# Moving the domain check of the weights from the first mixture into the second

## The chip, the cores and the metric

The kernel runs on one core of a Trainium2 chip. The metric is the device time of one execution in microseconds (us). The engines are TensorE (PE, with its weight loads PEld), VectorE (DVE), ScalarE (ACT), GpSimd (POOL) and SyncE (SP); in this kernel SP issues all DMAs, in the order of its own queue. Three runs of the kernel before gave a median of 1160.13 us (1159.07 to 1164.9).

## The reference

Three stages in float32: gated attention as a recurrence, and two mixtures of dense products.

```python
f = 1.0 / (1.0 + np.exp(-f_logit))              # 4 x 8 heads, 768 steps, 48 wide
state = f[:, :, t, :, None] * state + np.einsum('bhd,bhe->bhde', k[:, :, t], v[:, :, t])
y[:, :, t] = np.einsum('bhd,bhde->bhe', q[:, :, t], state)

h = x @ w_in                                    # x: 3072 x 384, w_in: 384 x 2048
x = (h * np.cos(h)) @ w_out                     # first mixture, w_out: 2048 x 384

xn = x / np.sqrt(np.mean(x * x, axis=-1, keepdims=True) + 1e-06) * rms_g
g, val = xn @ w_gate, xn @ w_val                # 384 x 1536 each
out = (g / (1.0 + np.exp(-g)) * val) @ w_out2   # second mixture, w_out2: 1536 x 384
```

The weights come as float64. The kernel reads them as 32-bit words and rebuilds each as two float32r parts by shifts. That holds only for magnitudes in a certain range, so every weight's upper word is also tested: this is the domain check. If a weight (or a gate product) is out of range, a general path at the end recomputes everything; with these inputs it does not run.

## The kernel before

Attention runs in 24 steps of 128 tokens, four pieces to a step. Both mixtures run over six blocks of 512 tokens, in slots. A slot of the first mixture takes one 128-wide slice of `w_in` (16 slots a block); one of the second takes a slice of the gate and value weights (12 a block). Slots are numbered through: 0 to 95 for the first mixture, 96 to 167 for the second. The pieces of attention lie in the slots of blocks 0 to 4 of the first mixture.

A slot of the first mixture is a chain over engines: nine matmuls into a bank (`m1_h`, L655), `kint` on ACT (L664), `wrap` on DVE (L670), the cosine on ACT (L676), `g` on DVE (L681), its two parts `gh` on ACT (L689) and `gl` on POOL (L697), and two slots later nine output matmuls (`m1_out`, L707). Banks alternate, so the matmuls of a slot wait for the `g` of two slots before. A slot of the second mixture has 18 matmuls (L805), `sg` on ACT (L814), `u` on DVE (L819), `uh` on ACT (L826), `ul` on DVE (L832) and 12 output matmuls of the slot before (L841).

The class `Decode` rebuilds weights. A unit is 128 x 384 weights: its words come by DMA into a `stage` tile (three buffers), ACT makes `wx` (L597), DVE joins the words in two steps (L609, L613), and ACT and POOL write the parts (L629, L630). The weights of the first mixture are decoded in the prologue and block 0, those of the second (36 units, `dec2`) in block 5 and in block 0 of the second mixture.

The domain check of one unit is one DVE instruction (L529), which folds the upper words into `wacc`:

```python
def domain(hi):
    nc.vector.scalar_tensor_tensor(
        out=wacc, in0=hi, scalar=1 << 30, in1=wacc, op0=ALU.bitwise_xor, op1=ALU.bitwise_and,
    )
```

For `w_in` and `w_out` the words are read a second time: `recheck` loads 32 units (L540) in slots 16 to 78 and checks each two slots later. For the 36 units of `dec2` the check follows L613. `count_ok` turns `wacc` into a flag, in slot 110.

What sets the order: `manual_schedule` keeps the order of the code in the prologue, in block 0, in block 5 (`blk5`) and from block 1 of the second mixture on (`ph1`). In blocks 1 to 4 of the first mixture (`mid`) and in block 0 of the second (`ph0`) a scheduler orders each engine's instructions by its own costs. Work that belongs to a slot number is put into tables: `post_at` (run at the key `po`), `dve_at` (at `dv`), `act_at`, `pe_at`. In `ph1` the keys run as `gv pe ok act sg dv u uh ul po out ev`, so on DVE `dv` stands ahead of `u`.

Per block the sums of squares go through memory: `ss_d` (L743), back as `ssc` (L745), and the inverse root is written as `ri_d` (L752), 512 values of 4 bytes. `norm` reads it back spread over the partitions (`rb`, L773) with `x2b` (L769) and scales on DVE (L780). The raw tiles of attention (f, k, q) come by L175 and L176 into three buffers and are turned on DVE (L180).

Of the kernel before, what the change touches and what calls it, by code (L numbers as in the profile page):

```python
# [32 lines left out]
def kernel(  # L33
# [15 lines left out]
    B, H, S, D = q.shape  # L49
# [7 lines left out]
    KD = DM // 128  # L57
    N1 = F1 // 128
    N2 = F2 // 128
# [3 lines left out]
    w_in_w, w_out_w, w_gate_w, w_val_w, w_out2_w = (  # L63
        w.bitcast(I32) for w in (w_in, w_out, w_gate, w_val, w_out2)
    )
    INV2PI = 1.0 / (2.0 * math.pi)

    # Attention runs in chunks of 128 tokens. With p(t) the running product of the gates in the
    # chunk and p_end its value at the chunk's end,
    #   y(t) = q(t) p(t)/p_end . [p_end S] + sum_{s<=t} (q(t) p(t)/p_end . k(s) p_end/p(s)) v(s).  # L70
    # Where p_end gets too small for that quotient the general path at the end recomputes
    # everything by the recurrence itself.
    # Dense products: every operand is the sum of two float32r parts. The weights come as the
    # words of float64; shifting an upper word left by 3 gives float32 bits of -|w| 2^128 (for
    # 2^-255 <= |w| < 1, what is outside goes to the general path), the lower word has the last
    # 3 bits.

    cpool = ctx.enter_context(tc.tile_pool(name="cpool", bufs=1))
    dpool = ctx.enter_context(tc.tile_pool(name="dpool", bufs=1, space=DRAM))
# [74 lines left out]
        for t in am + vtl + [Tz]:  # L154
            nc.gpsimd.memset(t, 0.0)

# [1 line left out]
    st = {}  # L158
    rawc = [0]

# [51 lines left out]
    def eng(x):  # L212
        return nc.vector if x == "V" else nc.gpsimd
# [94 lines left out]
    def att_bank():  # L308
        bc[0] += 1
        return bank[3 + bc[0] % 5] if bc[0] <= 5 * HEAD else bank[5 + bc[0] % 3]  # L310
# [4 lines left out]
    def copy(x):  # L315
        return nc.vector.tensor_copy if x == "V" else nc.scalar.copy

    def split(n, j):
        """Both parts of k and q of the pairs' heads j, one above the other."""
        kt, qt = st[n, "kt"], st[n, "qt"]  # L320
        top, bot, own = slice(0, D), slice(64, 64 + D), slice(64 * j, 64 * j + D)
        r = [copy(x) for x in OPT["rnd"]]
        if j == 0:
            r[0](out=ks[top], in_=kt[top])
            r[1](out=qs[top, 0], in_=qt[top])
            r[2](out=qs[bot, 0], in_=qt[top])
        else:
            r[3](out=ks[bot], in_=kt[bot])
            r[4](out=ks[top], in_=kt[bot])
            r[5](out=qs[bot, 0], in_=qt[bot])  # L330
            r[6](out=qs[top, 0], in_=qt[bot])
        eng(OPT["kl"][j]).tensor_tensor(
            out=ks[bot], in0=kt[own], in1=ks[own].bitcast(F32), op=ALU.subtract
        )
        eng(OPT["ql"][j]).tensor_tensor(
            out=qs[top, 1], in0=qt[own], in1=qs[own, 0].bitcast(F32), op=ALU.subtract
        )
# [70 lines left out]
    def ys(n):  # L408
        if True:
            t = att_bank()  # L410
            qt, vt, vt2 = st.pop((n, "qt")), st.pop((n, "v")), vtl[n % 2]
            inter = n % NCH > 0
            # Rows of x: 64 (i % 2) + 32 j + e of part i // 2 for e < 32, 16 (2 i + j) + e - 32 of
            # the last part for the others.
            for c in range(2):
                cs = slice(C * c, C * (c + 1))
                if inter:
                    for x in range(2):
                        i = 2 * c + x
                        nc.tensor.matmul(  # L420
                            t[64 * x:64 * x + 64, cs], Tz[:, i, 0:64], qt[:, i, :],
                            start=True, stop=False,
                        )
                for x in range(4):
                    i, j = divmod(4 * c + x, 2)
                    nc.tensor.matmul(
                        t[32 * x:32 * x + 32, cs], vt[:, 2 * i + j, 0:32],
                        am[j][:, C * i:C * (i + 1)], start=not inter, stop=True,
                    )
            if inter:  # L430
                for i in range(NP):
                    nc.tensor.matmul(
                        t[32 * i:32 * i + 32, 2 * C:3 * C], Tz[:, i, 64:96], qt[:, i, :],
                        start=True, stop=False,
                    )
            for j in range(2):
                for i in range(NP):
                    nc.tensor.matmul(
                        t[32 * i:32 * i + 32, 2 * C:3 * C], vt2[:, i, j:j + 2, :],
                        am[j][:, C * i:C * (i + 1)],  # L440
                        start=not inter and j == 0, stop=j == 1,
                    )
            st[n, "y"] = t
# [53 lines left out]
            Sn = st[n, "S"]  # L497
            nc.vector.tensor_tensor(out=Sn, in0=Sn, in1=z, op=ALU.add)

# [1 line left out]
    blocks = [(t0, 512) for t0 in range(0, NT, 512)]  # L501
    step_block = {}
    for j, (t0, n) in enumerate(blocks):
# [24 lines left out]
    def domain(hi):  # L528
        nc.vector.scalar_tensor_tensor(  # L529
            out=wacc, in0=hi, scalar=1 << 30, in1=wacc,  # L530
            op0=ALU.bitwise_xor, op1=ALU.bitwise_and,
        )

    def recheck_load(u):
        src = (w_in_w, w_out_w)[u % 2]
        R = src.shape[0] // 128
        words = src.rearrange("(p r) f -> p (r f)", r=R)
        n = 2 * KD * 128
        t = mp.tile([128, KD, 256], I32, tag="stage", name="stage", bufs=3)
        nc.sync.dma_start(  # L540
            out=t.rearrange("p c f -> p (c f)"), in_=words[:, n * (u // 2):n * (u // 2 + 1)]
        )
        return t[:, :, 1::2]

    class Decode:
        """Weights into pairs of float32r tiles, in steps that keep the engines apart."""

        def __init__(self, order, check):
            self.order, self.check = order, check
# [201 lines left out]
        nc.gpsimd.tensor_tensor(out=c, in0=c, in1=mh.to_broadcast([128, N // 128]), op=ALU.pow)  # L751
        nc.sync.dma_start(out=ri_d[t0:t0 + N].rearrange("(c p) -> p c", p=128), in_=c)  # L752

# [1 line left out]
    NB2 = NT // 512  # L755
    pairs2 = []
    o2 = [bank[0], bank[1], bank[2], bank[5]]
    pb = [(bank[6], bank[7]), (bank[3], bank[4])]
# [35 lines left out]
    pc = [0]  # L794
# [61 lines left out]
    mh = pp.tile([128, 1], F32, name="mh")  # L856

    def count_ok(b):
        """The partitions on which no gate product was too small and no weight out of range."""
        t = pp.tile([128, 4], F32, name="okt")  # L860
        ti = mp.tile([128, KD, 128], I32, tag="wx", name="oki", bufs=3)
        tf = mp.tile([128, KD, 128], F32, tag="stage", name="okf", bufs=3)
        nc.vector.tensor_scalar(
            ti, wacc, 26, 31, op0=ALU.logical_shift_right, op1=ALU.bitwise_and
        )
        nc.vector.tensor_scalar(tf, ti, 31.0, None, op0=ALU.is_equal)
        nc.vector.tensor_reduce(
            out=t[:, 0:1], in_=tf.rearrange("p c f -> p (c f)"), axis=AX.X, op=ALU.min
        )
        nc.vector.tensor_reduce(  # L870
            out=t[:, 1:2], in_=pall.rearrange("p n i -> p (n i)"), axis=AX.X, op=ALU.min
        )
        nc.vector.tensor_scalar(t[:, 2:3], t[:, 1:2], P_MIN, None, op0=ALU.is_ge)
        nc.vector.tensor_tensor(out=t[:, 3:4], in0=t[:, 0:1], in1=t[:, 2:3], op=ALU.mult)
        nc.vector.tensor_reduce(out=t[:, 1:2], in_=low, axis=AX.X, op=ALU.max)
        nc.vector.tensor_scalar(t[:, 2:3], t[:, 1:2], 0.0, None, op0=ALU.is_equal)
        nc.vector.tensor_tensor(out=t[:, 3:4], in0=t[:, 3:4], in1=t[:, 2:3], op=ALU.mult)
        nc.tensor.matmul(b[0:1, 0:1], t[:, 3:4], ones[:, 0:1], start=True, stop=True)
        nc.vector.tensor_copy(out=okn, in_=b[0:1, 0:1])
# [11 lines left out]
    if True:  # L891
# [72 lines left out]
        pe_at, act_at, post_at, dve_at = {}, {}, {}, {}  # L964

        def at(table, slot, fn, *a):
            table.setdefault(slot, []).append((fn, a))
# [7 lines left out]
        held = {}  # L975
# [5 lines left out]
        def set_(key, fn, *a):  # L981
            held[key] = fn(*a)

        def recheck(u, s):
            at(post_at, s, lambda: set_(("hi", u), recheck_load, u))
            at(dve_at, s + 2, lambda: domain(held.pop(("hi", u))))

        at(post_at, 12, lambda: nc.gpsimd.memset(ks.bitcast(F32), 0.0))
        at(post_at, 13, lambda: nc.gpsimd.memset(qs.bitcast(F32), 0.0))
        for u in range(2 * N1):  # L990
            recheck(u, N1 + 2 * u)

        def finish(j, s, short):
            at(act_at, s + (1 if short else 2), lambda: set_((j, "x2"), m1_evac, j))
# [15 lines left out]
        for j, (t0, N) in enumerate(blocks):  # L1010
# [3 lines left out]
            if final:  # L1014
# [15 lines left out]
                for u, key in enumerate(order2):  # L1030
# [3 lines left out]
                    else (w_gate_w if nm == "g" else w_val_w, None, 128 * i,  # L1034
                          lambda nm=nm, i=i: w2[nm, i])
                    for nm, i in order2
                ], True)
                norm(0, slot + 10)
            for i in range(N1):
                cur = []  # L1040
# [49 lines left out]
        for jj in range(NB2):  # L1090
# [4 lines left out]
            for i in range(N2):  # L1095
# [1 line left out]
                do = {  # L1097
                    "gv": lambda: m2_gv(jj, i),
                    "pe": lambda: run(pe_at, slot),
                    "ok": lambda: jj == 1 and i == 2 and count_ok(pb[pc[0] % 2][0]),  # L1100
                    "act": lambda: run(act_at, slot),
                    "t": lambda: jj == 0 and dec2.step_split(),
                    "x": lambda: jj == 0 and dec2.step_x(),
# [21 lines left out]
        stack2.close()  # L1125
    fast.close()

# [1 line left out]
    n_ok = nc.values_load(okn, min_val=0, max_val=128)  # L1129
    with tc.If(n_ok < 128):  # L1130
        general(
# [240 lines left out]
```

## Time and profile before

| | us |
|---|---|
| median of 3 runs | 1160.13 |
| profiled execution, span from the first to the last instruction | 1158.3 |
| PE busy | 1026.2 (89%) |
| DVE busy | 740.1 (64%) |
| ACT busy | 471.1 (41%) |
| POOL busy | 442.7 (38%) |

The page gives no time of the profiled execution beside its span; the median of the runs is 1.8 us above it, and that difference is taken for what lies around the span. The shares are means over stages that differ: the page's slices show DVE at 5 to 9 tenths over the first 65% of the span and at 2 to 3 tenths behind, while PE is at 9 tenths behind. In the stretches below, blocks are cut where the first L655 of a block starts (180.3, 291.7, 397.3, 498.0 and 591.6 us); 680.3 is the last `g` of the first mixture, and from 749.5 PE runs without a gap to 1147.6.

### The profile page before, as it was taken

How to read it: one execution, taken by the hardware profiler on the slowest of the kernel's cores; microseconds unless marked ns; L12 is line 12 of the kernel's file. 1: busy time of each engine (PE TensorE's matmuls, PEld its weight loads, DVE VectorE, ACT ScalarE, POOL GpSimd, SP SyncE). 2: the span in 40 equal slices, each digit the busy share in tenths (PEclk: the TensorE clock that was granted, in tenths of full speed). 3: DMA queues.
4: the chain of work that ended last, by engine and by line, in shares of the span. 5: the costliest groups of instructions: out<-in, count | busy, mean ns of one | idle time of the engine just before them, and what ended most of it. 6: DMA issues, size and time to landing. Idle time of an engine off the chain costs nothing.

```text
span 1158.3 us, 15494 instructions
## 1 busy us (share of the span) xinstructions
PE 1026.2 (89%) x5720; PEld 828.2 (71%) x5720; DVE 740.1 (64%) x1093; ACT 471.1 (41%) x841; POOL 442.7 (38%) x460
## 2 busy tenths in 40 slices
PE   6687789887987878998999787999999999999997
PEld 5455557665765666776776566788888888888886
DVE  6888999977895999887658699722322322323222
ACT  3355656444553555554555454422221222222211
POOL 3466676653654464656547556410000100001000
PEclk8697989998999899999999898999999999999999
DMA  9893353325425433530022434201010010100000
GB/s 160 175 181 104 91 144 100 91 26 131 126 60 98 141 113 100 89 88 1 2 68 69 105 121 147 83 18 47 1 64 1 1 65 1 64 1 1 28 1 31
DMA packets 108208, 84.90 MB, mean 73 GB/s; under 512 B 50518, under 2 KB 93526, under 8 KB 108124
## 3 DMA queue, kind: packets, MB, share of 16 engines
q1 hardware_dynamic: 108124, 83.82, 29.3%
q8 instruction: 47, 0.77, 0.3%
q14 instruction: 37, 0.30, 0.1%
HBM read 74.33 MB, written 9.46 MB: 72 GB/s over the span
## 4 chain that ended last, share of the span: by engine, by line
PE 43%; DVE 32%; DMA 9%; issue 8%; ACT 5%; SPq 1%; POOL 1%; DVEq 0%; ACTq 0%; POOLq 0%
PE bank L805 23%; PE bank L841 12%; PE bank L707 3%; DVE wrap L670 3%; DVE wx L609 3%; DVE g L681 3%; DVE wx L613 3%; DVE wacc L529 3%; PE bank L655 3%; DMA stage<-in_moe_w_out_dram 2%; DMA raw<-in_f_logit_dram 2%; DVE ft L271 1%; DVE E L253 1%; DVE ft L180 1%; DVE kt L180 1%
## 5 line engine op out<-in xcount | busy, mean ns | idle before, releaser
L707 PE MATMUL bank<-gh,wo 128*128 128x512 f32 x576 | 210.2, 420 | 2.3 <-ACT gh L689 2.3
L819 DVE SCALAR_TENSOR_TENSOR u<-bank,sg 128x512 f32<-128x512 f32 x72 | 49.7, 690 | 242.3 <-PE bank L805 240.8
L697 POOL TENSOR_TENSOR gl<-g,gh 128x512 fp32r<-128x512 f32 x96 | 133.4, 1390 | 124.0 <-ACT gh L689 119.0
L789 POOL TENSOR_TENSOR xl<-x2b,xh 128x512 fp32r<-128x512 f32 x18 | 24.5, 1366 | 314.3 <-ACT xh L788 314.3
L707 PEld LDWEIGHTS bank<-gh,wo 128*128 128x128 f32 x576 | 114.2, 198 | 31.8 <-issue 3.6
L707 PE MATMUL bank<-gl,wo 128*128 128x512 f32 x288 | 120.4, 418 | 10.7 <-POOL gl L697 10.7
L805 PE MATMUL bank<-xh,wo 128*128 128x512 f32 x360 | 122.8, 395 | 0.0
L814 ACT ACTIVATE sg<-bank 128x512 f32<-128x512 f32 x72 | 43.1, 598 | 168.9 <-PE bank L805 168.9
L676 ACT ACTIVATE wrap<-wrap,cb 128x512 f32<-128x512 f32 x96 | 69.4, 723 | 85.1 <-DVE wrap L670 84.5
L826 ACT CAST uh<-u 128x512 fp32r<-128x512 f32 x72 | 44.7, 621 | 142.8 <-DVE u L819 142.6
L689 ACT CAST gh<-g 128x512 fp32r<-128x512 f32 x96 | 59.4, 619 | 92.0 <-DVE g L681 69.5
L670 DVE SCALAR_TENSOR_TENSOR wrap<-bank,kint 128x512 f32<-128x512 f32 x96 | 65.4, 681 | 31.1 <-ACT kint L664 30.8
L832 DVE TENSOR_TENSOR ul<-u,uh 128x512 fp32r<-128x512 f32 x72 | 54.5, 757 | 44.7 <-ACT uh L826 44.7
L805 PEld LDWEIGHTS bank<-xh,wo 128*128 128x128 f32 x360 | 67.6, 188 | 14.6
L707 PEld LDWEIGHTS bank<-gl,wo 128*128 128x128 f32 x288 | 57.3, 199 | 26.1 <-POOL gl L697 15.6
L681 DVE SCALAR_TENSOR_TENSOR g<-bank,wrap 128x512 f32<-128x512 f32 x96 | 65.4, 681 | 16.1 <-ACT wrap L676 14.5
L841 PE MATMUL bank<-wo,uh 128*128 128x384 f32 x288 | 73.7, 337 | 0.0
L664 ACT ACTIVATE kint<-bank,cb 128x512 int32<-128x512 f32 x96 | 65.5, 683 | 15.6 <-PE bank L655 15.5
L805 PE MATMUL bank<-xl,wo 128*128 128x512 f32 x180 | 71.0, 394 | 0.0
L529 DVE SCALAR_TENSOR_TENSOR wacc<-stage,wacc 128x384 int32<-128x384 int32 x68 | 62.1, 913 | 11.5 <-DMA stage<-in_moe_w_in_dram 11.3
L841 PEld LDWEIGHTS bank<-wo,uh 128*128 128x128 f32 x288 | 52.6, 188 | 3.2 <-ACT uh L826 0.2
L613 DVE SCALAR_TENSOR_TENSOR wx<-stage,wx 128x384 int32<-128x384 int32 x52 | 51.8, 996 | 1.2
(376 smaller groups left out, 2506.9 us busy)
## 6 DMA issues: line engine op xcount, KB each, us to landing
stage<-in_moe_w_out_dram SPq DMA_DIRECT2D x44, 384.0 KB, 3.6
stage<-in_moe_w_in_dram SPq DMA_DIRECT2D x16, 384.0 KB, 3.9
v_sb<-in_v_dram SPq DMA_DIRECT2D x24, 192.0 KB, 4.2
x_d<-x SPq DMA_DIRECT2D x6, 768.0 KB
stage<-in_moe_w_gate_dram SPq DMA_DIRECT2D x12, 384.0 KB, 3.1
stage<-in_moe_w_val_dram SPq DMA_DIRECT2D x12, 384.0 KB, 3.3
x2b<-x_d SPq DMA_DIRECT2D x6, 768.0 KB, 5.0
out_dram<-ob SPq DMA_DIRECT2D x24, 192.0 KB, 2.0
```

The lines of the kernel that those rows point to most:

```text
L529: nc.vector.scalar_tensor_tensor(out=wacc, in0=hi, scalar=1 << 30, in1=wacc, op0=ALU.bitwise_xor, op1=ALU.bitwise_and,)
L613: nc.vector.scalar_tensor_tensor(out=f, in0=hi, scalar=-(1 << 29), in1=f, op0=ALU.bitwise_and, op1=ALU.bitwise_xor)
L664: nc.scalar.activation(out=kt, in_=hb[j, i], func=AF.Identity, scale=INV2PI * UNIT, bias=cb[:, 0:1])
L670: nc.vector.scalar_tensor_tensor(out=w, in0=hb[j, i], scalar=INV2PI * UNIT, in1=kt, op0=ALU.mult, op1=ALU.subtract)
L676: nc.scalar.activation(out=w, in_=w, func=AF.Sin, scale=2.0 * math.pi, bias=cb[:, 1:2])
L681: nc.vector.scalar_tensor_tensor(out=g, in0=hb.pop((j, i)), scalar=UNIT, in1=w, op0=ALU.mult, op1=ALU.mult)
L689: nc.scalar.copy(out=h, in_=g)
L697: e.tensor_tensor(out=l, in0=g, in1=h.bitcast(F32), op=ALU.subtract)
L707: nc.tensor.matmul(acc[m][:, 0:N], lw[:, cs], r, start=i == 0 and x == 0, stop=i == N1 - 1 and x == 2,)
L805: nc.tensor.matmul(t[y], l[:, 128 * kk:128 * (kk + 1)], r[:, kk, :], start=idx == 0, stop=idx == 3 * KD - 1,)
L832: nc.vector.tensor_tensor(out=l, in0=u, in1=h.bitcast(F32), op=ALU.subtract)
L841: nc.tensor.matmul(o2[tt][:, 0:DM], lu[:, cs], r, start=i == 0 and x == 0, stop=i == N2 - 1 and x == 2,)
```

## The change

All 68 checks are done in slots 108 to 157, which are blocks 1 to 4 of the second mixture and the first two slots of block 5. Each has a load of its own, of 384 KB from memory; `dec2` no longer checks, so the words of `w_gate`, `w_val` and `w_out2` are read twice. `count_ok` moves to slot 164. Line numbers behind the changed code are larger by 3. (The diff also empties comment lines.)

```diff
-    def recheck_load(u):
-        src = (w_in_w, w_out_w)[u % 2]
-        R = src.shape[0] // 128
-        words = src.rearrange("(p r) f -> p (r f)", r=R)
-        n = 2 * KD * 128
+    UNIT_W = 2 * KD * 128
+    units = [
+        (w, u) for w in (w_in_w, w_out_w, w_gate_w, w_val_w, w_out2_w)
+        for u in range(w.shape[0] * w.shape[1] // (128 * UNIT_W))
+    ]
+
+    def check_load(src, u):
+        words = src.rearrange("(p r) f -> p (r f)", r=src.shape[0] // 128)
         t = mp.tile([128, KD, 256], I32, tag="stage", name="stage", bufs=3)
         nc.sync.dma_start(
-            out=t.rearrange("p c f -> p (c f)"), in_=words[:, n * (u // 2):n * (u // 2 + 1)]
+            out=t.rearrange("p c f -> p (c f)"), in_=words[:, UNIT_W * u:UNIT_W * (u + 1)]
         )
         return t[:, :, 1::2]
...
-        def recheck(u, s):
-            at(post_at, s, lambda: set_(("hi", u), recheck_load, u))
-            at(dve_at, s + 2, lambda: domain(held.pop(("hi", u))))
-
...
-        for u in range(2 * N1):
-            recheck(u, N1 + 2 * u)
+
+        first = len(blocks) * N1 + N2
+        for n, (w, u) in enumerate(units):
+            s = first + n * (4 * N2) // len(units)
+            at(post_at, s, lambda n=n, w=w, u=u: set_(("hi", n), check_load, w, u))
+            at(dve_at, s + 2, lambda n=n: domain(held.pop(("hi", n))))
...
                     for nm, i in order2
-                ], True)
+                ], False)
...
-                    "ok": lambda: jj == 1 and i == 2 and count_ok(pb[pc[0] % 2][0]),
+                    "ok": lambda: jj == NB2 - 1 and i == 8 and count_ok(pb[pc[0] % 2][0]),
```

The scheduler of `mid` orders anew. On DVE in block 2 of the first mixture, where a step's q is done and the next step's f begins, stands before:

```order
L466 TENSOR_TENSOR xl_643<-bank_79,xh_642 128x3x128
L283 TENSOR_TENSOR qt<-qt,ft 128x512
L529 SCALAR_TENSOR_TENSOR wacc<-stage,wacc 128x384
L226 MEMSET ft 128x4
L180 STREAM_TRANSPOSE ft<-raw_128 128x4x4x32
```

and now:

```order
L466 TENSOR_TENSOR xl_643<-bank_79,xh_642 128x3x128
L283 TENSOR_TENSOR qt<-qt,ft 128x512
L226 MEMSET ft 128x4
L180 STREAM_TRANSPOSE ft<-raw_128 128x4x4x32
```

The check between the two steps is gone; the rest keeps its place. On SP in block 1, around the write of `ri_d` (L752, now L755), where raw_128 is the next step's f and raw_129 its k, stands before:

```order
L743 DMA ss_d<-ssr 1x512
L175 DMA raw_130<-in_q_dram 32x4x192
L176 DMA raw_130<-in_q_dram 32x4x160
L745 DMA ssc<-ss_d 128x4x1
L166 DMA v_sb<-in_v_dram 128x8x48
L175 DMA raw_128<-in_f_logit_dram 32x4x192
L752 DMA ri_d<-ssc 128x4x1
L176 DMA raw_128<-in_f_logit_dram 32x4x160
L175 DMA raw_128<-in_f_logit_dram 32x4x192
L176 DMA raw_128<-in_f_logit_dram 32x4x160
L540 DMA stage<-in_moe_w_in_dram 128x768
```

and now:

```order
L746 DMA ss_d<-ssr 1x512
L175 DMA raw_128<-in_f_logit_dram 32x4x192
L176 DMA raw_128<-in_f_logit_dram 32x4x160
L748 DMA ssc<-ss_d 128x4x1
L175 DMA raw_128<-in_f_logit_dram 32x4x192
L176 DMA raw_128<-in_f_logit_dram 32x4x160
L755 DMA ri_d<-ssc 128x4x1
L175 DMA raw_129<-in_k_dram 32x4x192
L176 DMA raw_129<-in_k_dram 32x4x160
```

Three of the four loads of f stood behind `ri_d`; now all four stand ahead of it and k follows it. On DVE in block 1 of the second mixture stands before:

```order
L832 TENSOR_TENSOR ul<-u,uh 128x512
L780 SCALAR_TENSOR_TENSOR x2b<-x2b,g_sb,rb 128x512
L819 SCALAR_TENSOR_TENSOR u<-bank_81,sg 128x512
L832 TENSOR_TENSOR ul<-u,uh 128x512
L780 SCALAR_TENSOR_TENSOR x2b<-x2b,g_sb,rb 128x512
L819 SCALAR_TENSOR_TENSOR u<-bank_78,sg 128x512
```

and now:

```order
L835 TENSOR_TENSOR ul<-u,uh 128x512
L529 SCALAR_TENSOR_TENSOR wacc<-stage,wacc 128x384
L783 SCALAR_TENSOR_TENSOR x2b<-x2b,g_sb,rb 128x512
L822 SCALAR_TENSOR_TENSOR u<-bank_81,sg 128x512
L835 TENSOR_TENSOR ul<-u,uh 128x512
L529 SCALAR_TENSOR_TENSOR wacc<-stage,wacc 128x384 x2
L783 SCALAR_TENSOR_TENSOR x2b<-x2b,g_sb,rb 128x512
L822 SCALAR_TENSOR_TENSOR u<-bank_78,sg 128x512
```

One or two checks stand in each slot between the `ul` of the slot before and the `u` of the slot.

## Rows read from the trace of the kernel before

**Rows 1.** Windows by stage: start:end length, busy per engine (instructions), PE clock, DMA share, GB/s

```profile
180.30:291.70 111.40, 92.24 (x566) 70.10 (x565) 95.92 (x145) 54.08 (x99) 57.72 (x61) 0.91 0.38 88
291.70:397.30 105.60, 89.10 (x580) 68.51 (x579) 87.97 (x145) 50.25 (x91) 60.33 (x64) 0.94 0.42 99
397.30:498.00 100.70, 88.90 (x560) 68.64 (x559) 89.69 (x142) 53.90 (x99) 57.42 (x60) 0.95 0.45 108
498.00:591.60 93.60, 86.11 (x571) 66.41 (x570) 68.28 (x106) 48.91 (x86) 51.51 (x55) 0.98 0.08 22
591.60:680.30 88.70, 77.67 (x314) 59.78 (x313) 66.85 (x83) 49.78 (x87) 54.31 (x42) 0.94 0.33 93
680.30:749.50 69.20, 55.69 (x236) 45.72 (x235) 62.04 (x84) 31.79 (x60) 34.98 (x28) 0.93 0.41 129
749.50:1147.60 398.10, 397.74 (x1903) 346.83 (x1903) 113.81 (x161) 90.26 (x154) 21.61 (x17) 1.00 0.07 21
```

**Rows 2.** The same windows for line L529 alone: length, DVE busy (instructions)

```profile
180.30:291.70 111.40, 4.71 (x6) 0.91 0.38 88
291.70:397.30 105.60, 9.04 (x13) 0.94 0.42 99
397.30:498.00 100.70, 6.93 (x9) 0.95 0.45 108
...
591.60:680.30 88.70, 21.98 (x16) 0.94 0.33 93
680.30:749.50 69.20, 17.79 (x21) 0.93 0.41 129
```

**Rows 3.** Timeline of block 5: start, duration, engine, line, operation, [idle before <-releaser]

```profile
639.73 0.68 DVE L670 SCALAR_TENSOR_TENSOR wrap<-bank,kint 128x512 f32<-128x512 f32 x1
...
642.75 1.42 POOL L697 TENSOR_TENSOR gl<-g,gh 128x512 fp32r<-128x512 f32 x1 [2.06 <-ACT gh L689]
...
642.94 1.65 DVE L529 SCALAR_TENSOR_TENSOR wacc<-stage,wacc 128x384 int32<-128x384 int32 x1
...
644.51 0.68 DVE L670 SCALAR_TENSOR_TENSOR wrap<-bank,kint 128x512 f32<-128x512 f32 x1
```

**Rows 4.** Waits of PE in block 1, then in block 2: total, times, longest

```profile
PE bank L655 <- DVE g L681: 6.8, 2, 5.7
...
PE bank L655 <- DVE g L681: 12.5, 2, 9.6
```

**Rows 5.** Timeline of DVE in block 1, then in block 2

```profile
263.91 1.11 DVE L180 STREAM_TRANSPOSE ft<-raw 128x512 f32<-128x512 f32 x1 [7.25 <-DMA raw<-in_f_logit_dram]
...
370.36 0.56 DVE L529 SCALAR_TENSOR_TENSOR wacc<-stage,wacc 128x384 int32<-128x384 int32 x1 [10.69 <-DMA stage<-in_moe_w_in_dram]
```

**Rows 6.** Chain of waits at the end of block 4: start, length, what

```profile
587.61 2.07 PE bank L655 x9
589.68 2.10 PE bank L707 x9
```

**Rows 7.** Timeline of DVE in block 5, slots that also scale `x2b`

```profile
662.11 0.75 DVE L780 SCALAR_TENSOR_TENSOR x2b<-x2b,g_sb,rb 128x512 f32<-128x512 f32 x1 [7.35 <-DMA rb<-ri_d]
...
666.97 0.68 DVE L670 SCALAR_TENSOR_TENSOR wrap<-bank,kint 128x512 f32<-128x512 f32 x1
...
672.75 0.68 DVE L670 SCALAR_TENSOR_TENSOR wrap<-bank,kint 128x512 f32<-128x512 f32 x1
```

**Rows 8.** Waits of PE from 680.3 to 749.5 us

```profile
PE bank L841 <- DVE ul L832: 5.9, 3, 2.5
PE bank L841 <- ACT uh L826: 4.0, 2, 3.5
```

**Rows 9.** Timeline of DVE in the second mixture, around 940 us

```profile
934.61 0.69 DVE L819 SCALAR_TENSOR_TENSOR u<-bank,sg 128x512 f32<-128x512 f32 x1 [3.23 <-PE bank L805]
...
940.88 0.69 DVE L819 SCALAR_TENSOR_TENSOR u<-bank,sg 128x512 f32<-128x512 f32 x1 [4.20 <-PE bank L805]
```

**Rows 10.** DMA issues by line: count, KB each, median us to landing

```profile
stage<-in_moe_w_in_dram SPq DMA_DIRECT2D x16, 384.0 KB, 3.9
```

## The prediction

> **What bounds the kernel now.** I cut the span into stages first, since its mean shares hide them [rows 1]. From 749.5 to 1147.6 us PE is busy 397.74 of 398.10 us at a granted clock of 1.00, and DVE only 113.81: that stretch is bound by PE, and DVE has 284 us to spare. Ahead of it the picture turns. In blocks 1 to 3 of the first mixture DVE is busy for 83 to 89% of the time, PE idles for 12 to 19 us in each, and the clock is 0.91 to 0.95. From 680.3 to 749.5 us DVE is busy 62.04 of 69.20 us, and PE idles for 13.5. So time taken from DVE ahead of 749.5 can shorten the kernel, and time given to it behind can be free.
>
> The second view is the same cut for the check alone [rows 2]: 4.71, 9.04 and 6.93 us in blocks 1, 2 and 3, 21.98 in block 5 and 17.79 in block 0 of the second mixture. Block 4 has no check, and is the shortest of the four. The third is the timeline of block 5, where the order is that of the code [rows 3]: from one `wrap` to the next it is 4.78 us, and the last 1.57 of them (642.94 to 644.51) are the check, which holds the next `wrap` back. The fourth is who waits. In blocks 1 and 2 the longest wait of PE on `g` is 5.7 and 9.6 us [rows 4], and DVE itself had stood before for 7.25 us for a load of f and for 10.69 us for the load of a check [rows 5].
>
> **What is removed, stage by stage.** I count a gain only where PE waits for DVE.
>
> Block 1: six checks, 4.71 us. DVE is busy for 86% of the block, but other waits of PE remain, so I take half: 2.4. The wait for f: three of its four loads stood behind the write of `ri_d` on SP, and now all stand ahead of it, so the 5.7 us that PE lost may go. But k now stands behind `ri_d` in their place and may be late instead, so of 5.7 I take 3. Together 5.4; the bounds are 0 and 5.7 + 4.7 = 10.4.
>
> Block 2: thirteen checks, half of 9.04 is 4.5. The check that waited 10.69 us for its own load goes. Behind it on DVE stood the turn of f and all else of the slot; PE lost 9.6 us. The turn of f ran at once when the check was done, so its own data was there. I count the whole 9.6: together 14.1, bounds 4.5 and 18.6. The upper end would leave the block at 87.0, below the 93.6 of block 4, so I cut it to 12.0 + 4, that is 16.
>
> Block 3: half of 6.93, 3.5; bounds 0 and 7. Block 4: nothing to remove. Blocks 1 to 3: 23.0.
>
> Block 5: without the check a slot of DVE is 4.78 − 1.57 = 3.21 us. Then PE is late next: nine matmuls of 2.07 and nine of 2.10 us, 4.17 [rows 6]. So a slot gains 4.78 − 4.17 = 0.61, not 1.57; thirteen slots give 7.9. Three slots also scale `x2b` and last 5.78 (666.97 to 672.75) [rows 7]; without the check they come to 4.21, so 1.57 each, 4.7. From 12.6 I take off two things. The first scaling waits 7.35 us for `rb`, which is loaded two slots ahead of it; with quicker slots it waits some 1.2 us more. And POOL, busy for 54 of 88.7 us, has the squares of block 4 to do in the first slots of this block besides, so that `gl` can be late there; with no row for it I take 3. That leaves 8.4; bounds 5 and 12.6.
>
> Here a rule speaks against the change. The check lasts 0.56 us in one row [rows 5] and 1.65 in block 5, beside a POOL instruction that runs from 642.75 to 644.17 [rows 3]. The Trainium skill, page "SBUF — State Buffer", section "Who interferes with whom", says that a VectorE instruction with two inputs from SBUF and a GpSimd instruction that reads SBUF shut each other out for the whole instruction; the two rows agree. By that rule 1.09 us of the check is a wait for `gl`, and L609 or L613, which have two such inputs too, would inherit it: a DVE slot would be an estimated 3.21 + 1.09 = 4.30 us, 0.13 above PE's, and the sum would lose 16 x 0.13 = 2.1.
>
> Block 0 of the second mixture: 21 checks, 17.79 us of a DVE that is 90% busy. PE waited 5.9 us for `ul` and 4.0 for `uh` [rows 8], both behind `u` on the full DVE. I take 9 of these 9.9; bounds 5 and the 13.5 that PE idles in all.
>
> The sum is 23.0 + 8.4 + 9 = 40.4.
>
> **What is added.** 68 checks and 68 loads in 48 slots, 1.42 a slot and never more than two. A slot there is 6.27 us (934.61 to 940.88), and DVE idles 4.20 us ahead of `u`, or 3.23 where it also writes the output [rows 9]. In the order the checks stand in that very gap. Two of them cost 1.1 us at 0.56 or 3.3 at 1.65; POOL is busy for only 21.61 of 398 us, so I take 0.56: 68 x 0.56 = 38 us in 284, on the path nothing. If the cover were gone, 38 us would be the price, and 112 at 1.65.
>
> The checks also add a wait for a load, with `u`, then `uh`, `ul` and PE's L841 queued behind it. A load is asked for when the check three units earlier has freed its buffer, some two slots (12.5 us) ahead of its use, and such a load now lands in 3.9 us [rows 10]. On SP the loads stand among those of `x2b` and `rb`, which are asked for two slots ahead of use as well; a check load that waits for its buffer holds them for part of a slot. I count nothing. Memory traffic grows by 36 loads, 14 MB: the stretch moves 21 GB/s, and 68 loads of 384 KB over 301 us add an estimated 89, together about what block 3 moves, where PE was not held by it. `count_ok` does the same instructions in another slot bound by PE: nothing, as now.
>
> The span of the profiled execution is 1158.3; less 40.4 is 1117.9, and with the 1.8 us around it the time is 1119.7: 1120.
>
> **Rivals.** (a) *The DMA waits of the first mixture stay under another name.* The write of `ri_d` still falls once in each block, and raw loads still pass through the same queue. For it: two different loads were hit in blocks 1 and 2. Against it: block 3 has the same write and its DVE did not stand for a load. Then 3 + 9.6 us are not gained, 1132; and if block 3 is hit as well, 9.6 more, 1142. I price it at 1137.
>
> (b) *Everything falls to PE's pace.* Blocks 1 to 3 come down to the 93.6 of block 4, which is 17.8 + 12.0 + 7.1 = 36.9; block 5 gives 12.6 and block 0 13.5. Sum 63, time 1097. Against it: block 4 has less attention work on DVE (68.28 us busy).
>
> (c) *The second mixture waits for the checks' loads: the slower side.* Its place is DVE ahead of `u` in blocks 1 to 4. With three buffers, three loads must go round in 3 x 301/68 = 13.3 us, landing plus check. Up to a landing of 12.7 us nothing is lost. From there each us costs 68/3 = 23 us; at 14.5 the gain is eaten, from 14.8 on it is slower. At 16 it is 68/3 x 16.56 − 301 = 74 us: 1194. For it: the load of rows 5 was over 10 us late. Against it: that was behind a write of `ri_d`, and none of those falls into these blocks (the last belongs to slot 106); 3.9 is the median.
>
> (d) *The check is not in the way.* DVE's other waits end at the same time, and little is gained: 5 us, 1155. Against it: in rows 3 nothing but the check separates L613 from the next `wrap`.
>
> **How the numbers follow.** Forecast (1120, some 10 us to either side) 0.58; (a) 0.22; (b) 0.12; (c) 0.06, of which 0.04 slower and 0.02 no change; (d) 0.02. What differs by less than 0.5% (5.8 us) can't be told from no change. Faster is 0.58 + 0.22 + 0.12 = 0.92, no change 0.04, slower 0.04. The range reaches from the upper half of (b), 1102, to the far end of (a), 1143; it leaves out half of (b), (c) and (d), some 0.14.
>
> **What would show it.** Right: no L529 ahead of 749.5; `wrap` to `wrap` in block 5 at 4.2 to 4.3 us; block 2 near 92 us with no load wait of 10 us on DVE; the stretch of PE without a gap begins near 709 us and lasts 398 us as now; L529 near 0.56 us in idle time of DVE. Wrong: a wait of DVE for `stage` ahead of `u` with a hole on PE behind it (c); a wait of 5 us or more for a raw tile in blocks 1 to 4 (a); slots in block 5 still near 4.8 us because POOL or ACT is late (d).

## The result and the profile after

The changed kernel takes 1115.74 us (median of 4 runs, 1114.17 to 1117.8), the kernel before 1159.6 us beside it (4 runs). The ratio is 0.9621, with a 95% interval of 0.9596 to 0.9645. The forecast was 1120. The profiled execution has a span of 1112.4 us and a time of 1114.52, so 2.1 us lie around the span.

The same cut by stages as in [rows 1], for the changed kernel: start:end length, busy us of PE, PEld, DVE, ACT and POOL, granted PE clock, DMA share, GB/s.

```profile
57.70:175.50 117.80, 91.51 (x577) 65.92 (x577) 108.78 (x141) 69.98 (x127) 78.61 (x78) 0.94 0.53 131
175.50:275.80 100.30, 88.62 (x568) 68.20 (x569) 92.14 (x142) 54.03 (x98) 56.38 (x61) 0.95 0.34 73
275.80:371.20 95.40, 86.96 (x580) 67.39 (x578) 81.45 (x133) 51.95 (x95) 57.14 (x64) 0.98 0.28 60
371.20:469.50 98.30, 88.74 (x560) 68.74 (x559) 85.85 (x133) 53.66 (x97) 54.58 (x60) 0.95 0.31 64
469.50:562.30 92.80, 86.48 (x571) 66.46 (x570) 67.03 (x105) 47.77 (x84) 51.74 (x55) 0.98 0.08 20
562.30:642.40 80.10, 71.90 (x304) 57.77 (x303) 48.12 (x67) 50.28 (x87) 51.98 (x42) 0.96 0.36 97
642.40:703.80 61.40, 54.08 (x244) 45.12 (x243) 48.33 (x63) 31.33 (x60) 34.43 (x29) 0.97 0.51 159
703.80:1106.20 402.40, 402.37 (x1929) 351.25 (x1927) 153.47 (x232) 91.28 (x157) 21.59 (x17) 1.00 0.28 86
```

The last window is longer than that of [rows 1] because the cut behind block 0 falls elsewhere, at the last 402.4 us of PE's matmuls. The old kernel cut so (749.5 to 1151.87) has the same 402.4. The stages in order:

| stage | before | after | difference | forecast |
|---|---|---|---|---|
| start and block 0 | 180.3 | 175.5 | −4.8 | 0 |
| block 1 | 111.4 | 100.3 | −11.1 | −5.4 |
| block 2 | 105.6 | 95.4 | −10.2 | −14.1 |
| block 3 | 100.7 | 98.3 | −2.4 | −3.5 |
| block 4 | 93.6 | 92.8 | −0.8 | 0 |
| block 5 | 88.7 | 80.1 | −8.6 | −8.4 |
| block 0 of the second mixture | 69.2 | 61.4 | −7.8 | −9 |
| from there on | 402.4 | 402.4 | 0 | 0 |

The six stages from block 1 to block 0 of the second mixture gave 11.1 + 10.2 + 2.4 + 0.8 + 8.6 + 7.8 = 40.9 us, where 40.4 was forecast. The span is shorter by 45.9, the median by 43.9.

Where [rows 3] had a check between `g` and `wrap`, the timeline of block 5 now reads (start, duration, engine, line, operation, [idle before <- releaser]):

```profile
604.36 0.69 DVE L673 SCALAR_TENSOR_TENSOR wrap<-bank,kint 128x512 f32<-128x512 f32 x1 [0.27 <-ACT kint L667]
...
605.91 0.69 DVE L684 SCALAR_TENSOR_TENSOR g<-bank,wrap 128x512 f32<-128x512 f32 x1 [0.86 <-ACT wrap L679]
606.52 0.55 DVE L612 SCALAR_TENSOR_TENSOR wx<-stage,wx 128x384 int32<-128x384 int32 x1
607.11 0.56 DVE L616 SCALAR_TENSOR_TENSOR wx<-stage,wx 128x384 int32<-128x384 int32 x1
607.40 1.43 POOL L700 TENSOR_TENSOR gl<-g,gh 128x512 fp32r<-128x512 f32 x1 [1.17 <-ACT gh L692]
607.94 0.69 DVE L673 SCALAR_TENSOR_TENSOR wrap<-bank,kint 128x512 f32<-128x512 f32 x1 [0.27 <-ACT kint L667]
```

From `wrap` to `wrap` it is 3.58 us here, and DVE idles in front of three of its instructions: it no longer sets the slot. (This slot follows a longer one; over twelve slots, from the `wrap` at 565.37 to that at 615.87 us, the mean is 4.21.) The chain of waits there (start, length, what) shows who does, and what comes next:

```profile
602.53 2.10 PE bank L710 x9
604.63 2.07 PE bank L658 x9
606.71 2.10 PE bank L710 x9
...
612.52 15.47 DMA rb<-ri_d
```

PE runs its 18 matmuls in 4.18 us without a gap, and then the load of `rb` takes over, for 15.47 us. The first scaling of `x2b` waits longer for it than in [rows 7], 11.56 us against 7.35:

```profile
611.56 0.37 SPq L755 DMA_DIRECT2D ri_d<-ssc  x1
...
612.52 0.48 SPq L776 DMA_DIRECT2D rb<-ri_d  x1
...
628.12 0.75 DVE L783 SCALAR_TENSOR_TENSOR x2b<-x2b,g_sb,rb 128x512 f32<-128x512 f32 x1 [11.56 <-DMA rb<-ri_d]
```

In block 5 PE loses 8.2 us to that and next to nothing to POOL (total, times, longest):

```profile
PE bank L658 <- DVE g L684: 8.2, 1, 8.2
...
PEld bank L710 <- POOL gl L700: 0.2, 1, 0.2
```

All waits of DVE for a DMA in the changed kernel are these three. The one for f lies ahead of block 1; the waits of [rows 5] have nothing in their place:

```profile
DVE x2b L783 <- DMA rb<-ri_d: 11.6, 1, 11.6
DVE ft L180 <- DMA raw<-in_f_logit_dram: 4.6, 1, 4.6
DVE x2b L783 <- DMA x2b<-x_d: 1.8, 1, 1.8
```

In the second mixture the checks stand in the idle time in front of `u` (the first row of the next fence groups all 68: least, median and longest ns, first and last start):

```profile
L529 DVE SCALAR_TENSOR_TENSOR wacc<-stage,wacc x68: 548/552/1676, 740.2 to 1035.7; 128x384 int32<-128x384 int32 x68
```

```profile
739.55 0.69 DVE L835 TENSOR_TENSOR ul<-u,uh 128x512 fp32r<-128x512 f32 x1 [0.69 <-ACT uh L829]
740.16 1.15 DVE L529 SCALAR_TENSOR_TENSOR wacc<-stage,wacc 128x384 int32<-128x384 int32 x2
744.44 0.69 DVE L822 SCALAR_TENSOR_TENSOR u<-bank,sg 128x512 f32<-128x512 f32 x1 [3.14 <-PE bank L808]
```

With two checks in the slot DVE still idles 3.14 us before `u` and waits for PE. PE is busy for 402.37 of the 402.40 us at a granted clock of 1.00.

### The profile page after: what moved, and what is told of

It is laid out like the page before. It is cut to its first block, busy times and chain, and to the rows that moved or that the text cites. A ratio compares the mean times of both kernels' runs of the same rounds, so it can differ in the third digit from the quotient of the medians.

```text
span 1112.4 us, 15586 instructions
## 1 busy us (share of the span) xinstructions
PE 1006.1 (90%) x5720; PEld 817.5 (73%) x5720; DVE 727.2 (65%) x1093; ACT 470.3 (42%) x841; POOL 431.9 (39%) x460
## 4 chain that ended last, share of the span: by engine, by line
PE 49%; DVE 28%; DMA 8%; issue 7%; ACT 5%; SPq 2%; POOL 1%; DVEq 0%; ACTq 0%; POOLq 0%
PE bank L808 24%; PE bank L844 13%; PE bank L710 5%; PE bank L658 4%; DVE g L684 3%; DVE wrap L673 3%; DVE wx L612 2%; DVE E L253 2%; DVE wx L616 2%; DMA raw_in<-in_moe_w_in_dram 2%; DMA rb<-ri_d 1%; DVE kt L180 1%; DVE ft L180 1%; DMA raw<-in_k_dram 1%; DVE am L355 1%
## 5 line engine op out<-in xcount | busy, mean ns | idle before, releaser
L700 POOL TENSOR_TENSOR gl<-g,gh 128x512 fp32r<-128x512 f32 x96 | 129.2, 1346 | 134.6 <-ACT gh L692 125.9
L710 PE MATMUL bank<-gl,wo 128*128 128x512 f32 x288 | 119.5, 415 | 11.4 <-POOL gl L700 11.4
L835 DVE TENSOR_TENSOR ul<-u,uh 128x512 fp32r<-128x512 f32 x72 | 52.2, 724 | 45.4 <-ACT uh L829 45.4
L667 ACT ACTIVATE kint<-bank,cb 128x512 int32<-128x512 f32 x96 | 65.5, 683 | 15.0 <-PE bank L658 13.5
L616 DVE SCALAR_TENSOR_TENSOR wx<-stage,wx 128x384 int32<-128x384 int32 x52 | 51.4, 993 | 1.5
L529 DVE SCALAR_TENSOR_TENSOR wacc<-stage,wacc 128x384 int32<-128x384 int32 x68 | 51.1, 751 | 0.7
```

What stands on the lines that cost most here:

```text
L529: nc.vector.scalar_tensor_tensor(out=wacc, in0=hi, scalar=1 << 30, in1=wacc, op0=ALU.bitwise_xor, op1=ALU.bitwise_and,)
L616: nc.vector.scalar_tensor_tensor(out=f, in0=hi, scalar=-(1 << 29), in1=f, op0=ALU.bitwise_and, op1=ALU.bitwise_xor)
L667: nc.scalar.activation(out=kt, in_=hb[j, i], func=AF.Identity, scale=INV2PI * UNIT, bias=cb[:, 0:1])
L700: e.tensor_tensor(out=l, in0=g, in1=h.bitcast(F32), op=ALU.subtract)
L710: nc.tensor.matmul(acc[m][:, 0:N], lw[:, cs], r, start=i == 0 and x == 0, stop=i == N1 - 1 and x == 2,)
L835: nc.vector.tensor_tensor(out=l, in0=u, in1=h.bitcast(F32), op=ALU.subtract)
```

## The experiments

The theory behind them was that the gain has two independent sources of some 20 us each: the checks and loads of `w_in` and `w_out` that leave the first mixture, and the checks of `dec2` that leave block 5 and block 0; and that the second mixture does the work for nothing. In the first mixture the loads count most, because those that SP issues behind the write of `ri_d` come late. The rivals: DVE's time counts and the loads don't; the checks are not free in the second mixture. Ratios below are to the kernel before, timed beside each kernel.

### Each half of the change alone

`e1_dec2_only` does the checks of `dec2` late and keeps those of `w_in` and `w_out` where they were. `e2_first_only` is the other half. Both are edits of the changed kernel.

```diff
 # e1_dec2_only
-        (w, u) for w in (w_in_w, w_out_w, w_gate_w, w_val_w, w_out2_w)
+        (w, u) for w in (w_gate_w, w_val_w, w_out2_w)
...
+        for u in range(2 * N1):
+            recheck(u, N1 + 2 * u)
```

```diff
 # e2_first_only
-        (w, u) for w in (w_in_w, w_out_w, w_gate_w, w_val_w, w_out2_w)
+        (w, u) for w in (w_in_w, w_out_w)
...
-                ], False)
+                ], True)
```

Expected: 

> Only the 36 checks of the second mixture's weights move (with loads of their own); the 32 re-read checks of w_in and w_out stay in the first mixture. Theory (each stage gives what VectorE holds back there): blocks 1 to 4 of the first mixture as before, block 5 and block 0 of the second mixture shorter by 8.6 + 7.8 us as in the changed kernel, so about 16 us under the kernel before, 1143. Rival (the gain comes from the loads and waits of the first mixture alone): within 5 us of the kernel before, 1155 to 1160.

> Only the 32 checks of w_in and w_out move into the second mixture; the 36 units of the second mixture's weights are checked where they are decoded, as before. Theory: blocks 1 to 3 give the 24 us that they gave in the changed kernel, block 5 and the block behind it nothing: about 25 us under before, 1135. Rival (parts overlap, either alone gives most of it): 1120.

Measured: 1139.06 us, ratio 0.9832 (0.9811 to 0.9853); and 1134.23 us, 0.9793 (0.9774 to 0.9813). At 1159.6 that is −19.5 and −24.0 us, together −43.5; the whole change gives −43.9. (For e1 some 16 us had been expected.) The two halves add up and don't hide each other. The traces put them where they belong: blocks 1 to 4 take 411.3 us before, 410.6 in e1, 387.6 in e2 and 386.8 after; from the start of block 5 to the end it is 566.7 before, 548.7 in e1, 568.2 in e2 and 550.1 after. These sums repeat within some 1.5 us where the code is the same. A single block does not: blocks 1 to 4 of e1 differ from before by −2.3, +1.7, +1.3 and −1.4, so a term for one block is known to some 3 us.

### No check at all

`e3_no_check` leaves the whole domain check out.

```diff
-        for n, (w, u) in enumerate(units):
+        for n, (w, u) in enumerate([]):
```

Expected: 

> No check of the weights at all: neither the 68 loads nor the 68 instructions (this part of the computation is left out). Theory (the second mixture hides the check fully): the time of the changed kernel within 3 us, 1113 to 1118. Rival (the loads or the checks cost something there, hidden by a gain elsewhere): 1105 or less.

Measured: 1112.37 us, ratio 0.9624 (0.9594 to 0.9654), against 0.9621 with all checks. The two can't be told apart, but their intervals together leave some 0.4% open. The traces are closer: blocks 1 to 4 of the second mixture, from one block's first matmul on `wi0h` to the same four blocks later, take 300.85 us after (735.86 to 1036.71) and 300.85 here (733.44 to 1034.29). The second mixture hides 68 checks and 68 loads of 384 KB.

### In the first mixture: the loads or DVE's time

`e4_loads_first` adds to the changed kernel the 32 loads at their old places, with one column of each copied on DVE in place of the check. `e5_dve_first` adds 32 instructions of the check's form on data already there, and no load.

```diff
 # e4_loads_first
+    tiny = pp.tile([128, 1], I32, name="tiny")
...
+        def recheck(u, s):
+            src = (w_in_w, w_out_w)[u % 2]
+            at(post_at, s, lambda: set_(("hi", -u - 1), check_load, src, u // 2))
+            at(dve_at, s + 2, lambda: nc.vector.tensor_copy(
+                out=tiny, in_=held.pop(("hi", -u - 1))[:, 0, 0:1]
+            ))
+
+        for u in range(2 * N1):
+            recheck(u, N1 + 2 * u)
```

```diff
 # e5_dve_first
+        def busy(u):
+            domain(gp[2][:, 0:DM].bitcast(I32).rearrange("p (c f) -> p c f", c=KD))
+
+        for u in range(2 * N1):
+            at(dve_at, N1 + 2 * u + 2, busy, u)
+        at(dve_at, len(blocks) * N1 + 4, lambda: nc.vector.memset(wacc, -1))
```

Expected: 

> The changed kernel, with the 32 loads of w_in and w_out words put back into the first mixture as well; each is read by a copy of one column in the place of the check, so the loads and the waits for them are back, but not the 0.56 to 1.65 us of VectorE. Theory for blocks 1 to 3: two thirds of their 24 us were the waits for loads (7 and 10 us), so some 13 to 18 us come back, time about 1130. Rival (it was VectorE's busy time that held the blocks back): within 5 us of the changed kernel, 1116 to 1121.

> The changed kernel, with 32 extra instructions of the form of the check on VectorE in blocks 1 to 4 of the first mixture, one every two slots, which read the g of the slot before in place of loaded words; no load and no wait for one comes with them. Theory (waits for loads were most of the gain there): a third or less of the 24 us comes back, 1118 to 1124. Rival (VectorE's busy time was): 12 to 24 us come back, 1128 to 1140.

Measured: 1130.9 us, ratio 0.9758 (0.9732 to 0.9783); and 1127.03 us, 0.9733 (0.9688 to 0.9778). Blocks 1 to 4 as one window, of the kernel after, then of e4 and of e5:

```profile
175.50:562.30 386.80, 350.80 (x2273) 270.79 (x2274) 326.47 (x510) 207.41 (x373) 219.84 (x240) 0.96 0.25 55
```

```profile
179.50:582.20 402.70, 356.26 (x2273) 274.50 (x2274) 327.05 (x538) 207.97 (x373) 224.26 (x240) 0.94 0.35 83
```

```profile
175.90:574.10 398.20, 354.51 (x2274) 273.01 (x2275) 346.69 (x541) 208.05 (x373) 220.43 (x240) 0.95 0.25 53
```

Without the checks the loads cost 15.9 us, with DVE's busy time as after (327.05 against 326.47). DVE's time alone costs 11.4 us for 20.2 us of work. Together they cost 24.5 (411.3 − 386.8), not 27.3. The difference of 2.8 us is at the edge of what sums that repeat within 1.5 us can show; part of DVE's work may fit into the waits. So both theories are half right: e5's 1127.03 lies above the theory's range and below the rival's. These 15.9 us need not be the traffic of the loads alone. With the loads back the scheduler again puts three of f's four loads behind `ri_d` (249.68 to 251.13 us, the write 249.26), as it did before the change; no run separates the two. In e4 both waits of [rows 5] are back, one for f and one for the load, though no check is there:

```profile
261.26 1.10 DVE L181 STREAM_TRANSPOSE ft<-raw 128x512 f32<-128x512 f32 x1 [7.11 <-DMA raw<-in_f_logit_dram]
...
365.18 0.15 DVE L994 COPY tiny<-stage 128x1 int32<-128x1 int32 x1 [9.68 <-DMA stage<-in_moe_w_in_dram]
```

### How much the second mixture can hide

Each check four times (`e6_check_x4`), six times (`e6_check_x6`), and once but one slot after its load was asked for in place of two (`e7_one_slot`).

```diff
 # e6_check_x4; x6 has 6 in place of 4
-            at(dve_at, s + 2, lambda n=n: domain(held.pop(("hi", n))))
+            at(dve_at, s + 2, lambda n=n: [domain(held["hi", n]) for _ in range(4)])
```

```diff
 # e7_one_slot
-            at(dve_at, s + 2, lambda n=n: domain(held.pop(("hi", n))))
+            at(dve_at, s + 1, lambda n=n: domain(held.pop(("hi", n))))
```

Expected: 

> The changed kernel with each check in the second mixture done four times: 272 instructions, 3.1 us of VectorE a slot on average, in slots with two units 4.4 us, against the 4.2 that VectorE idled ahead of u. Theory (they run in idle time right behind ul): 0 to 5 us slower than the changed kernel. Rival (the checks already hold u back a little): 3 x 51 us of extra VectorE time show for a good part, 1150 or more.

> As before, six times: 408 instructions, 4.7 us a slot, 6.6 in the 20 slots with two units, 3.3 in the 28 with one. Theory: the slots with two units overrun the 4.2 us of idle time by 2.4 us each and more where GpSimd or the scaling stands in the way, 20 x 2.4 = 48, of which the slot of one unit behind it gives some back since PE runs one slot of output matmuls ahead: 20 to 60 us slower, 1135 to 1175. Rival (VectorE's order has slack over two slots): no loss, 1116 to 1120.

> The changed kernel with each check one slot behind its load in place of two. Theory (loads land in about 4 us, a slot is 6.27): same time within 3 us; VectorE waits for a load at most in the slots where x2b and rb are loaded too. Rival (the loads land late, over 10 us, and two slots were needed): VectorE stands before u, PE has holes, 1130 or more.

Measured: 1116.95 us, 0.9644 (0.9604 to 0.9683); 1169.8 us, 1.0099 (1.0067 to 1.0131); 1115.15 us, 0.9632 (0.9591 to 0.9674). Four times the checks cost nothing that can be measured; six times cost 54 us and make the kernel slower than before. The window from 740 us on shows why, first of four times, then of six, and then the first 60 us of six:

```profile
740.00:1040.00 300.00, 300.00 (x1437) 262.20 (x1436) 235.92 (x388) 66.87 (x115) 15.64 (x12) 1.00 0.38 110
```

```profile
740.00:1100.00 360.00, 328.19 (x1469) 277.44 (x1469) 311.55 (x525) 65.19 (x118) 15.60 (x12) 0.96 0.31 92
```

```profile
740.00:800.00 60.00, 55.68 (x260) 46.93 (x260) 52.32 (x90) 10.78 (x19) 2.05 (x2) 1.00 0.32 97
```

At four PE has no hole. At six PE idles for 31.8 of 360 us, and the matmuls take 328.19 / 1469 = 0.2234 us each in place of 300.00 / 1437 = 0.2088: 21.5 us more over 1469. The two are 53.3 of the 54. The granted clock falls to 0.96, but not all of the 21.5 goes with it: in the first 60 us it is still 1.00, and between the holes a matmul takes 55.68 / 260 = 0.2142 there. That difference alone would be an estimated 8 us over 1469, which leaves some 13.5 for the lower clock. The timeline of DVE, and then the waits, of six:

```profile
806.48 8.20 DVE L529 SCALAR_TENSOR_TENSOR wacc<-stage,wacc 128x384 int32<-128x384 int32 x12
814.61 0.68 DVE L822 SCALAR_TENSOR_TENSOR u<-bank,sg 128x512 f32<-128x512 f32 x1
```

```profile
PE bank L844 <- ACT uh L829: 29.9, 15, 2.8
...
ACT uh L829 <- DVE u L822: 279.9, 47, 9.1
```

Twelve checks last 8.20 us, more than the 6.27 of a slot; `u` follows with no idle time, `uh` waits up to 9.1 us for it and PE for `uh`. One slot of lead is enough for a load: in e7 DVE never waits for `stage`.

### The write of `ri_d`

In the kernel after, `norm(0)` asks for `rb` right behind the write of `ri_d`. `e8_norm_early` asks three slots earlier, ahead of that write. `e9_ri_on_act` issues the write from ACT in place of SP. `e10_before_ri_on_act` does the same in the kernel before. `e11_both` is e8 and e9 together.

```diff
 # e8_norm_early, e11_both
-                norm(0, slot + 10)
+                norm(0, slot + 7)
```

```diff
 # e9_ri_on_act, e11_both; in the kernel before: e10_before_ri_on_act
-        nc.sync.dma_start(out=ri_d[t0:t0 + N].rearrange("(c p) -> p c", p=128), in_=c)
+        nc.scalar.dma_start(out=ri_d[t0:t0 + N].rearrange("(c p) -> p c", p=128), in_=c)
```

Expected: 

> The changed kernel with the loads of x2b and rb for block 0 of the second mixture, and its scaling, three slots earlier in block 5, so that on the queue they stand ahead of the writes of ss_d and ri_d of that block. The changed kernel's VectorE waits 11.56 us for rb there and PE loses 8.2. Theory (rb is late because it stands behind the write of ri_d): the wait goes, block 5 is 6 to 9 us shorter, 1107 to 1110. Rival (rb itself takes 12 us or more, being one row read 128 times): the wait stays, since the scaling comes three slots earlier too, 1114 to 1118.

> The changed kernel with the write of ri_d issued by ScalarE's queue in place of SyncE's. Theory (loads on SyncE's queue are held because they follow ri_d in the same queue): rb and the raw tiles are no longer late, 5 to 9 us faster, 1107 to 1111. Rival (the write of 512 values of 4 bytes holds the DMA engines, whoever issues it, or rb is slow by itself): same time within 4 us, the wait for rb still about 11 us.

> The kernel before, its checks where they were, with the write of ri_d issued by ScalarE's queue. Theory (the waits of 7.2 and 10.7 us in blocks 1 and 2 and of 7.4 us for rb were loads held behind ri_d in SyncE's queue, not the checks): those waits go, blocks 1 to 4 are some 16 us shorter and block 5 some 7, 1135 to 1140. Rival (the checks' loads themselves overload the queue): waits for loads of 7 us or more remain in blocks 1 and 2, 1150 or more.

> The changed kernel with both edits of the last call: ri_d on ScalarE's queue, and x2b, rb and the scaling three slots earlier. Theory (both take away the same wait for rb): no more than either alone, 1105 to 1108. Rival (the earlier scaling also takes work out of the crowded end of block 5): 1101 or less.

Measured: e8 1108.33 us, 0.9574 (0.9557 to 0.9592); e9 1106.17 us, 0.9552 (0.9533 to 0.9572); e11 1109.13 us, 0.956 (0.9525 to 0.9594); e10 1142.11 us, 0.9854 (0.9826 to 0.9881). The first three beat the kernel after and can't be told apart (e9 lies 0.8 us under its expected range, e11 1.1 above); both edits together give no more than one, so they cure the same wait. In e8 the load of `rb` (of block 0, whose values were written long before) is issued 15.7 us ahead of that write of `ri_d`, and the scaling starts with no wait:

```profile
598.09 0.48 SPq L776 DMA_DIRECT2D rb<-ri_d  x1
...
605.61 0.83 DVE L783 SCALAR_TENSOR_TENSOR x2b<-x2b,g_sb,rb 128x512 f32<-128x512 f32 x1
...
613.84 0.37 SPq L755 DMA_DIRECT2D ri_d<-ssc  x1
```

From issue to that start it is 7.5 us, against the 15.47 to landing in the kernel after, so `rb` isn't slow by itself; and the write is still in SP's queue, so the order alone cures the wait. In e9 `rb` is issued before `ri_d` as well (611.43 and 614.31), so it doesn't show whether ACT's queue adds anything. For the waits of [rows 5] e10 tells more. These are all its waits of DVE for a DMA:

```profile
DVE ft L180 <- DMA raw<-in_f_logit_dram: 3.5, 1, 3.5
DVE x2b L780 <- DMA x2b<-x_d: 2.9, 1, 2.9
DVE wacc L529 <- DMA stage<-in_moe_w_out_dram: 2.1, 1, 2.1
DVE x2b L780 <- DMA rb<-ri_d: 0.5, 1, 0.5
```

The 7.25 and the 10.69 are gone. In block 1 every load keeps its place in SP's queue and only the write leaves it, so the write in that queue was the cause of f's wait. In block 2 the scheduler also moved the load that had been late: it was issued at 358.08 us, behind the write at 356.83, and is issued at 338.22 in e10, ahead even of the load of `ssc`. That fits the same cause, but is no test of the queue. How the write held f's loads in the kernel before is seen on SP (first its waits for the values of all six writes, then the issues in block 1):

```profile
SPq L752 <- POOL ssc L751: 31.7, 6, 10.9
```

```profile
240.24 0.53 SPq L175 DMA_DIRECT2D raw<-in_f_logit_dram  x1
251.74 0.37 SPq L752 DMA_DIRECT2D ri_d<-ssc  x1
252.15 0.50 SPq L176 DMA_DIRECT2D raw<-in_f_logit_dram  x1
```

SP stood for 10.9 us until POOL had the values to be written, with three loads of f behind. The last of these was issued at 253.50, and DVE turned f at 263.91, some 10 us later, where loads of f land in 2.2 to 2.6 us in the median. So the loads were late twice: they were issued late, and they landed slowly. In e10 SP issues all four between 235.65 and 237.19.

From block 5 to the end e10 is 7.0 us shorter than before (559.7 for 566.7), as expected. But blocks 1 to 4 are only 8.3 us shorter (403.0) in place of 16, and 1142.11 lies above the 1135 to 1140 expected. That DVE, with the checks still there, is busy in the time that it no longer waits would explain it; no run shows it by itself.

## Why the prediction was right

**Blocks 1 and 2.** 21.3 us came where 19.5 were forecast, but split otherwise. In block 1 the step that failed is "of 5.7 I take 3": k behind `ri_d` was not late, the wait went whole, and the gain passed even the upper bound of 10.4, by less than the 3 us to which a block is known. In block 2 it is the sum of the whole wait (9.6) and half of the checks (4.5). Each was sized about right by itself: block 2 is 102.8 us in e4 and 100.3 in e5, 7.4 and 4.9 more than after. Yet both together give 10.2. A slot that stands for a late load also has room for checks, so the two terms may overlap. Over the four blocks that overlap is 15.9 + 11.4 − 24.5 = 2.8 us, for block 2 alone 2.1; neither is clear of the scatter. That the two blocks together came within 2 us of the forecast is in part luck, since one gave more and the other less.

**Half of DVE's check time.** For 20.2 us of DVE work in blocks 1 to 4, e5 shows 11.4 us, 0.56 of it. The half was a good guess.

**Block 5.** The sum of 8.4 is right (8.6) by two errors that cancel. On DVE's chain the thirteenth `wrap` comes 8.9 us earlier in the block than before (at 615.87, before at 654.08), where 7.9 were counted, and the three slots that scale `x2b` give 3.9 for 4.7. I took 3 us off for a late `gl`; PE waited 0.2 us for it. And I gave the wait for `rb` 1.2 us more; it became 4.2 longer. That wait stood in [rows 7], and its reason was not followed up: `rb` is issued right behind `ri_d` (647.84 and 646.88 us before), the very order that I had made the cause of the waits of [rows 5]. Without it the kernel is some 5 to 8 us faster by the ratios (e8, e9).

**The rule against the change** applied, but cost PE nothing. By it (the Trainium skill, page "SBUF — State Buffer", section "Who interferes with whom") L612 or L616 would have had to wait for `gl`. In the rows above they have started before `gl` and last 0.55 and 0.56 us; what then runs beside `gl` is `wrap`, with one input from PSUM, and it lasts 0.69. Not every slot is so. L616 lasts 1.26 to 1.65 us in 7 of its 15 instructions of the block, each time beside a POOL instruction that began first, and once that is `gl`:

```profile
580.92 1.29 POOL L700 TENSOR_TENSOR gl<-g,gh 128x512 fp32r<-128x512 f32 x1 [0.40 <-ACT gh L692]
...
580.98 1.65 DVE L616 SCALAR_TENSOR_TENSOR wx<-stage,wx 128x384 int32<-128x384 int32 x1
```

From `wrap` to `wrap` that slot takes 4.67 us (577.89 to 582.56), above PE's 4.18. But in the whole block PE waited for `g` only once, the 8.2 us behind `rb`, so the 2.1 us by the rule were not lost. A check that meets a POOL instruction which reads SBUF shows the rule too, in the second mixture:

```profile
790.26 1.31 POOL L792 TENSOR_TENSOR xl<-x2b,xh 128x512 fp32r<-128x512 f32 x1 [4.95 <-ACT xh L791]
790.31 1.68 DVE L529 SCALAR_TENSOR_TENSOR wacc<-stage,wacc 128x384 int32<-128x384 int32 x1
```

The check takes 1.68 us there and 0.55 by itself. All 68 take 51.05 us, where the estimate was 38, and the room held that too.

**Block 0 of the second mixture and the rest.** 7.8 for 9, and nothing for nothing. e1 gives 19.5 us for these checks in both stages, against 8.4 + 9 = 17.4; e2 gives 24.0 for the others, against 23.0.

**The first 180 us** were 4.8 us shorter, which no step had. Only three checks go there, some 1.6 us. The same code takes 178.5 us in e1 and 176.5 in e10, so most of it is one execution against another: the granted clock was 0.77 ahead of block 0 and 0.89 in it before, 0.82 and 0.94 after. Why it differs is open. It explains why the span shrank by 5 us more than the sum, and the medians by 3.5.

**The rivals.** (a) fell: no raw tile of blocks 1 to 4 was late. It was a near miss: in e4, with the loads of the checks back in SP's queue and f's behind `ri_d` again, f is late by 7.11 us. And one wait of this kind did stay, that for `rb` in block 5. (b) fell: blocks 1 to 3 stay at 95 to 100 us. (c) fell: no hole on PE, and e7 shows that half of the lead was enough. (d) fell by e1 and e2.

## What to carry to other kernels

Read an engine's spare time by stage, not from its mean share: the same 68 checks, 32 of them with a load of their own, cost 44 us in one place and nothing in another, and the room there held four times as many but not six times. A tiny scattered write (512 values of 4 bytes) in the queue that also brings the loads made those behind it some ten us late here, in one case by the wait for its values as well: ask for the loads first, or try another queue for the write. And when two costs sit in the same slot, a late load and an engine's work, test each alone: removing both may give back less than their sum.

## What the runs showed of the hardware

- A load issued behind the write of `ri_d` in SP's queue made DVE wait 7.1 to 11.6 us in blocks 1, 2 and 5 (before and e4 in all three, after in block 5); in block 3 no such wait was seen. Moving only the write to ACT's queue removed it in block 1 (e10), and asking for `rb` ahead of the write removed it in block 5 (e8). In block 1 before, SP stood 10.9 us ahead of the write, and the loads behind took some 10 us more to land. What makes them land slowly was not separated.
- The wait for `rb` grew when everything ahead of it got faster, from 7.35 to 11.56 us: the load, 14.1 us from issue before and 15.47 after, did not come sooner when DVE did.
- The cover ends between four and six checks in place of one (five was not run): with four nothing is lost, with six 54 us. Of these 31.8 are holes of PE, and an estimated 13.5 go with the granted clock, which is 0.96 over the stretch with the holes and 1.00 in the one without.
- A check, with both inputs in SBUF, lasts 0.55 us by itself and 1.65 to 1.68 beside a POOL instruction of 1.31 to 1.42 us that reads SBUF; `wrap`, with one input from PSUM, keeps its 0.69.
